# Retention, softplus layer and squared-ReLU layer on one core: the same chunk of two sequences in one visit

## The chip, the core and the metric

The kernel runs on one core of a Trainium2 chip. TensorE (PE) multiplies, VectorE (DVE), ScalarE (ACT) and GpSimd (POOL) work elementwise, and SyncE (SP) issues the DMAs. The metric is the device time of one execution in microseconds; the median of three runs before is 874.35 us.

## The reference

Three layers follow one another on 2304 tokens (4 sequences of 576) of width 512 (8 heads of 64).

```python
scores = scale * np.matmul(q, k.transpose(0, 1, 3, 2))       # (4, 8, 576, 576)
gamma = 1.0 - 2.0 ** (-5.0 - np.arange(H, dtype=np.float32))
Dmat = np.where(rel >= 0, gamma[:, None, None] ** rel[None, :, :], 0.0)
x = np.matmul(scores * Dmat, v)                              # then (2304, 512)
h = x @ w_in                                                 # w_in 512 x 2048
g = np.maximum(h, 0.0) + np.log1p(np.exp(-np.abs(h)))
x = g @ w_out                                                # w_out 2048 x 512
h = x @ w_in2
r = np.maximum(h, 0.0)
out = (r * r) @ w_out2
```

## The kernel before

**Retention.** Each sequence has 9 chunks of 64 tokens, 36 in all. A chunk tile `ch` holds q, k and v in three slots of 128 partitions: on the lower half (LO) q and k with the head's 64 dimensions on partitions and, in the third slot, the state; on the upper half (HI) k and v with tokens on partitions, and the masked products in the first slot. `step_s` (line 317) makes for each of 8 heads two 64x64 products: pb = k q (line 326; contraction over rows LO, output on columns HI) and, but for a sequence's last chunk, the running state st += k v (line 332; rows HI, columns LO). DVE masks pb into the chunk tile (line 336), ACT copies the state to the next chunk's tile (line 338). `step_o` (line 340) makes po of the same 8 heads (line 348), over all 128 rows, with even heads on columns LO and odd heads on HI, and DVE multiplies it with the decay table xw (line 361). A 64x64 product stands as two records of PE in the trace. The quadrant of a product follows from the partitions of its operands and of its output: rows LO or HI, columns LO or HI.

**First layer.** Tokens are cut into five tiles of 512, 384, 512, 512 and 384. A step is one of 16 blocks of w_in: `g1` (12 matmuls into a PSUM bank ph, line 401), softplus on ACT (lines 415 to 417) and DVE (lines 422, 425, 428, the last one reads ph), the split of its result (lines 437, 438), and two steps later `g2` (12 matmuls, line 453). During the steps of a tile, `attend` (line 757) visits the chunks of the next tile: one visit is step_o of the chunk before, the load of a chunk ahead, step_s of this chunk and the scaling of a loaded v (line 311). It stands between g1 of a step and g2 of an earlier one. The weights are converted on ACT and DVE (lines 140, 141, 145, 173, 174), all of the first layer's during the first tile, the second layer's w_in later.

**Start.** The chunks of tile 0 and one more are worked off before the first g1, in the order in which the code is written (`manual_schedule`, line 717); elsewhere a scheduler orders the instructions of each engine, and the engines take them in that order. PSUM has eight banks: four `ps_acc`, two `ps_h` (ph by turns), one `ps_at` (po), one `ps_st`. In the steady visits pb and st lie in the one bank of ps_st, pb on partitions HI and st on LO (line 324).

**Second layer.** From about 480 us on (lines 545 and 564), it reads the first layer's result back from DRAM and writes 18 output tiles of 128x512 (line 464).

## Time and profile before

| | |
|---|---|
| runs | 874.32, 874.35, 878.71 us; median 874.35 |
| span of the profiled execution | 871.7 us, 2.65 below the median; its own time outside the span is not recorded |
| PE busy | 858.3 us (98%) |
| DVE, ACT, POOL busy | 579.7, 422.2, 8.8 us |
| chain that ended last | PE 83%, DMA 6%, DVE 4%, ACT 4% |
| po, pb and st | 576, 576 and 512 records |

The span runs from the first to the last instruction. Busy time is the union of an engine's instructions, so a PE that is busy may still hold short matmuls that follow one another at less than its best pace; for them the starts in the timeline say more than the busy share. A record of a 512-wide matmul is longer (0.39 us) than the distance to the next start, since matmuls are pipelined.

### The profile page before, as it was taken

Reading aid. Unit: us, or ns where it says so; the run is one execution under the profiler, and the core shown is the slowest. Engines: PE = TensorE matmul, PEld = TensorE weight load, DVE = VectorE, ACT = ScalarE, POOL = GpSimd, SP = SyncE. Lnnn points to the kernel's source line nnn. Section 1 sums busy time; section 2 is a strip of 40 time slices with the busy share of each in tenths; the row PEclk is TensorE's granted clock in tenths of the full one; section 3 lists DMA queues with packets and bytes.
Section 4 is the critical chain, followed back from the end, with each engine's and each line's share of the span. In section 5 each row is a group of like instructions: output and inputs, shape, how many; then the busy total and the mean of one; then the engine's idle time right before and its main releaser. Section 6 shows DMA issues by size and latency. Waiting matters only on the chain.

```text
span 871.7 us, 14212 instructions
## 1 busy us (share of the span) xinstructions
PE 858.3 (98%) x5520; PEld 754.4 (87%) x5520; DVE 579.7 (67%) x1002; ACT 422.2 (48%) x763; POOL 8.8 (1%) x12
## 2 busy tenths in 40 slices
PE   8899999999999999999999999999999999999998
PEld 7777888999888888888999989888888988998896
DVE  3799899977896578745788874447645446553544
ACT  2599997665675446644696561213322113221121
POOL 2100000000000000000000000000000000000000
PEclk9999999999999999999999999999999999999999
DMA  9867764861583117610432464436644343644442
GB/s 209 229 181 211 220 210 148 246 203 50 165 264 104 30 45 239 221 36 1 170 115 55 149 226 121 120 110 193 193 115 115 121 118 115 191 120 115 116 121 85
DMA packets 75766, 126.32 MB, mean 145 GB/s; under 512 B 6706, under 2 KB 41650, under 8 KB 75698
## 3 DMA queue, kind: packets, MB, share of 16 engines
q1 hardware_dynamic: 75700, 125.42, 48.7%
q8 instruction: 44, 0.72, 0.3%
q14 instruction: 22, 0.18, 0.1%
HBM read 101.28 MB, written 24.12 MB: 144 GB/s over the span
## 4 chain that ended last, share of the span: by engine, by line
PE 83%; DMA 6%; DVE 4%; ACT 4%; issue 1%; SPq 0%; POOL 0%; DVEq 0%; ACTq 0%
PE acc L564 23%; PE acc L453 18%; PE ph L401 18%; PE py L545 9%; PE px L545 6%; PE pz L545 6%; PE st L326 2%; DMA wo_raw<-in_moe_w_out_dram 2%; DMA ch<-in_kv_dram 2%; PE po L348 2%; DMA wi_raw<-in_moe_w_in_dram 1%; DVE ct L145 1%; PE st L332 1%; DMA ch<-in_qk_t_dram 1%; ACT e L416 1%
## 5 line engine op out<-in xcount | busy, mean ns | idle before, releaser
L401 PE MATMUL ph<-xh,wi 128*128 128x512 f32 (+1 forms) x640 | 146.2, 369 | 2.9 <-DVE e L428 2.1
L401 PEld LDWEIGHTS ph<-xh,wi 128*128 128x128 f32 x640 | 116.3, 188 | 19.9 <-DVE e L428 2.2
L453 PE MATMUL acc<-gh,woh 128*128 128x512 f32 (+1 forms) x320 | 120.5, 378 | 0.0
L453 PE MATMUL acc<-gl,woh 128*128 128x512 f32 (+1 forms) x320 | 117.8, 368 | 0.2 <-DVE gl L438 0.2
L453 PE MATMUL acc<-gh,wol 128*128 128x512 f32 (+1 forms) x320 | 117.8, 368 | 0.0
L564 PE MATMUL acc<-woh,gring 128*128 128x512 f32 x288 | 104.9, 393 | 0.0
L545 PE MATMUL py<-t,sring 128*128 128x384 f32 x432 | 86.9, 335 | 0.3 <-DVE uring L652 0.3
L545 PEld LDWEIGHTS py<-t,sring 128*128 128x128 f32 x432 | 77.2, 188 | 6.8 <-DVE uring L652 0.6
L437 ACT CAST gh<-e 128x512 fp32r<-128x512 f32 (+1 forms) x80 | 45.8, 573 | 71.6 <-DVE e L428 54.2
L401 PE MATMUL ph<-xl,wi 128*128 128x512 f32 (+1 forms) x320 | 78.7, 367 | 0.0
L422 DVE SCALAR_TENSOR_TENSOR e<-e 128x512 f32<-128x512 f32 (+1 forms) x80 | 50.9, 636 | 38.0 <-ACT l L417 37.2
L438 DVE TENSOR_TENSOR gl<-e,gh 128x512 fp32r<-128x512 f32 (+1 forms) x80 | 50.9, 636 | 29.1 <-ACT gh L437 28.6
L453 PEld LDWEIGHTS acc<-gh,woh 128*128 128x128 f32 x320 | 60.0, 188 | 8.9 <-ACT gh L437 0.2
L453 PEld LDWEIGHTS acc<-gh,wol 128*128 128x128 f32 x320 | 60.1, 188 | 7.9
L590 ACT CAST gh<-g 128x384 fp32r<-128x384 f32 x48 | 24.6, 513 | 86.8 <-DVE g L577 72.1
L453 PEld LDWEIGHTS acc<-gl,woh 128*128 128x128 f32 x320 | 60.1, 188 | 7.5 <-DVE gl L438 0.4
L401 PEld LDWEIGHTS ph<-xl,wi 128*128 128x128 f32 x320 | 58.7, 188 | 7.6
L590 ACT CAST gring<-g 128x384 fp32r<-128x384 f32 x48 | 24.6, 513 | 83.0 <-DVE g L577 83.0
L415 ACT ACTIVATE e<-ph 128x512 f32<-128x512 f32 (+1 forms) x80 | 44.0, 550 | 37.3 <-PE ph L401 37.1
L564 PEld LDWEIGHTS acc<-woh,gring 128*128 128x128 f32 x288 | 54.0, 188 | 9.2
L545 PE MATMUL px<-t,sring 128*128 128x384 f32 x288 | 58.3, 337 | 0.0
L545 PE MATMUL pz<-t,sring 128*128 128x384 f32 x288 | 58.2, 337 | 0.0
...
## 6 DMA issues: line engine op xcount, KB each, us to landing
...
```

Of the source, the lines that this page charges most:

```text
L145: nc.vector.scalar_tensor_tensor(out=ct, in0=up, scalar=3, in1=low, op0=ALU.logical_shift_left, op1=ALU.bitwise_or,)
L326: nc.tensor.matmul(pb[HI, h, :], lhsT=kk[LO, h, :], rhs=qp[LO, h, :], start=True, stop=True, skip_group_check=True,)
L348: nc.tensor.matmul(po[(LO, HI)[h % 2], h // 2, :], lhsT=sv[rows, h, :], rhs=qp[rows, h, :], start=True, stop=True, skip_group_check=True,)
L401: nc.tensor.matmul(ph[:, :n], lhsT=a, rhs=x, start=(j == 0), stop=(j == len(todo) - 1))
L415: nc.scalar.activation(out=e, in_=ph[:, :n], func=AF.Abs)
L422: nc.vector.scalar_tensor_tensor(out=e, in0=e, scalar=-2.0, in1=e, op0=ALU.add, op1=ALU.mult)
L437: nc.scalar.copy(h[:, :n], g)
L438: nc.vector.tensor_tensor(out=l[:, :n], in0=g, in1=h[:, :n], op=ALU.subtract)
L453: nc.tensor.matmul(acc[j][:, :n], lhsT=a, rhs=x, start=(begin and m == 0), stop=(end and m == 2))
L545: nc.tensor.matmul(ps, lhsT=a, rhs=x, start=(first and m == 0), stop=(m == len(todo) - 1), skip_group_check=True,)
L564: nc.tensor.matmul(acc2[j, m], lhsT=a, rhs=x, start=(begin and n == 0), stop=(end and n == 2))
L590: nc.scalar.copy(h, g)
```

## The change

A visit takes chunk c of sequences 2s and 2s+1 together, so there are 18 visits, and the tokens stand in that order (64 of one sequence, 64 of the other) through both layers; each output tile is put back by two DMAs of 64 rows. The chunk tile has both sequences side by side, the load buffers are two pairs in place of three chunks. step_s splits the heads: heads 0 to 3 give pb on columns HI and st on LO, heads 4 to 7 pb on LO and st on HI, so that the four kinds of products lie on four quadrants. The state fills its bank; pb goes to the bank that the next ph will have (`pb_next`), in the start to one of ps_acc. Mask and state copy are two instructions of 64x512 per pair. The table xw is no longer made for all chunks at the start but just before each step_o (`make_xw`, into `xw_now`).

```diff
--- before.py
+++ after.py
@@ -18,7 +18,7 @@
 D = 64
 CN = 64
 SCN = 9
-LOADS = 3
+LOADS = 2
 STAGES = 3
 EARLY = {"wi": 9, "wo": 8}
...
@@ -89,20 +91,20 @@
     ew = ctx.enter_context(tc.tile_pool(name="ew", bufs=2))
     gp = ctx.enter_context(tc.tile_pool(name="gp", bufs=2))
     at = ctx.enter_context(tc.tile_pool(name="at", bufs=LOADS))
-    n_first = TILES[0][1] // CN
+    n_first = TILES[0][1] // P
     first = tc.tile_pool(name="first", bufs=n_first)
     first_pool = first.__enter__()
     late_wts = []
     ps_acc = ctx.enter_context(tc.tile_pool(name="ps_acc", bufs=4, space=PSUM))
-    ps_h = ctx.enter_context(tc.tile_pool(name="ps_h", bufs=2, space=PSUM))
+    ps_h = ctx.enter_context(tc.tile_pool(name="ps_h", bufs=1, space=PSUM))
     ps_at = ctx.enter_context(tc.tile_pool(name="ps_at", bufs=1, space=PSUM))
     ps_st = ctx.enter_context(tc.tile_pool(name="ps_st", bufs=1, space=PSUM))
     dram = ctx.enter_context(tc.tile_pool(name="dram", bufs=1, space=DRAM))
-    cst = const.tile([P, C_ALL], F32, name="cst")
+    cst = const.tile([P, C_T + 4 * (SCN - 1)], F32, name="cst")
     below_one = cst[:, C_ONE:C_ONE + 1]
     round_up = cst[:, C_UP:C_UP + 1]
-    mask = cst[CN:P, C_MASK:C_MASK + CN].unsqueeze(1).to_broadcast([CN, H, CN])
+    mask = cst[:, C_MASK:C_MASK + CN].unsqueeze(1).to_broadcast([P, H, CN])
     x2d = dram.tile([KD, P, NT], F32, name="x2d")
     NP = KF // 2
     KH = KD // 2
@@ -290,82 +292,113 @@
     LO, HI = slice(0, P // 2), slice(P // 2, P)
+    def place(c, s):
+        return (c // SCH * 2 + s) * SCH + c % SCH
+
+    def new_chunk(c):
+        if c < NPR:
+            pool = first_pool if c < n_first else at
+            chunk[c] = pool.tile([P, 3, 2, H, CN], F32, tag="ch", name="ch")
+
     def load_qk(c):
-        if c < NCH:
-            pool = first_pool if c < n_first else at
-            chunk[c] = pool.tile([P, 3, H, CN], F32, tag="ch", name="ch")
-            nc.sync.dma_start(out=chunk[c][LO, 0:2], in_=qk_t[c])
+        if c < NPR:
+            if c not in chunk:
+                new_chunk(c)
+            for s in range(2):
+                nc.sync.dma_start(out=chunk[c][LO, 0:2, s], in_=qk_t[place(c, s)])
     def load_kv(c):
-        if c < NCH:
-            nc.sync.dma_start(out=chunk[c][HI, 1:3], in_=kv[c])
+        if c < NPR:
+            for s in range(2):
+                nc.sync.dma_start(out=chunk[c][HI, 1:3, s], in_=kv[place(c, s)])
     def load_chunk(c):
         load_qk(c)
         load_kv(c)
     def scale_v(c, eng=nc.vector):
-        if c < NCH:
+        if c < NPR:
             t = chunk[c][HI, 2]
             w = cst[HI, C_VW + c % SCH * H:C_VW + (c % SCH + 1) * H]
             eng.tensor_tensor(
-                out=t, in0=t, in1=w.unsqueeze(2).to_broadcast([CN, H, D]), op=ALU.mult
+                out=t, in0=t, op=ALU.mult,
+                in1=w.unsqueeze(1).unsqueeze(3).to_broadcast([CN, 2, H, D]),
             )
     state = []
-
-    def step_s(c, split):
+    HH = H // 2
+
+
+
+
+    def step_s(c, pb):
         qp, kk, sv = (chunk[c][:, i] for i in range(3))
         go_on = c % SCH < SCH - 1
         if c % SCH == 0:
-            state[:] = [ps_st.tile([P, H, D], F32, tag="st", name="st")]
+            state[:] = [ps_st.tile([P, 2, HH, D], F32, tag="st", name="st")]
         st = state[0]
-        pb = st if not split else ps_acc.tile([P, H, CN], F32, tag="at", name="pb")
-        for h in range(H):
-            nc.tensor.matmul(
-                pb[HI, h, :], lhsT=kk[LO, h, :], rhs=qp[LO, h, :],
-                start=True, stop=True, skip_group_check=True,
-            )
-            if go_on:
-
-                nc.tensor.matmul(
-                    st[LO, h, :], lhsT=kk[HI, h, :], rhs=sv[HI, h, :],
-                    start=c % SCH == 0 and h == 0, stop=True, skip_group_check=True,
-                )
-        nc.vector.tensor_tensor(out=qp[HI], in0=pb[HI], in1=mask, op=ALU.mult)
+        for s in range(2):
+            for h in range(HH):
+                for to, hh in ((HI, h), (LO, h + HH)):
+                    nc.tensor.matmul(
+                        pb[to, s * HH + h, :], lhsT=kk[LO, s, hh, :], rhs=qp[LO, s, hh, :],
+                        start=True, stop=True, skip_group_check=True,
+                    )
+                if go_on:
+                    for to, hh in ((LO, h), (HI, h + HH)):
+                        nc.tensor.matmul(
+                            st[to, s, h, :], lhsT=kk[HI, s, hh, :], rhs=sv[HI, s, hh, :],
+                            start=c % SCH == s == h == 0, stop=True, skip_group_check=True,
+                        )
+        for of, i in ((HI, 0), (LO, 1)):
+            nc.vector.tensor_tensor(
+                out=qp[HI, :, i * HH:(i + 1) * HH],
+                in0=pb[of].rearrange("p (s h) c -> p s h c", s=2),
+                in1=mask[of].rearrange("p (s h) c -> p s h c", s=2), op=ALU.mult,
+            )
         if go_on:
-            nc.scalar.copy(chunk[c + 1][LO, 2], st[LO])
+            for of, i in ((LO, 0), (HI, 1)):
+                nc.scalar.copy(chunk[c + 1][LO, 2, :, i * HH:(i + 1) * HH], st[of])
+
+    def pb_acc():
+        return ps_acc.tile([P, H, CN], F32, tag="at", name="pb")
     def step_o(c, ps):
         qkv = chunk.pop(c)
         qp, sv = qkv[:, 0], qkv[:, 2]
         rows = slice(0, P) if c % SCH else HI
-        xw = cst[:, C_XW + c % SCH * 256:C_XW + (c % SCH + 1) * 256]
-        xw = xw.rearrange("p (a b) -> p a b", a=KD)
-        po = ps.tile([P, H, CN], F32, tag="at", name="po")[:, 0:KD, :]
-        for h in range(H):
-            nc.tensor.matmul(
-                po[(LO, HI)[h % 2], h // 2, :], lhsT=sv[rows, h, :], rhs=qp[rows, h, :],
-                start=True, stop=True, skip_group_check=True,
-            )
-        t, off = tile_of(c * CN)
+        xw = xw_first if c % SCH == 0 else xw_now
+        xw = xw.rearrange("p (a b) -> p a b", a=KD).unsqueeze(1).to_broadcast([P, 2, KD, CN])
+        po = ps.tile([P, H, CN], F32, tag="at", name="po").rearrange(
+            "p (s a) b -> p s a b", s=2
+        )
+        if c % SCH:
+            make_xw(c % SCH)
+        for s in range(2):
+            for h in range(H):
+                nc.tensor.matmul(
+                    po[(LO, HI)[h % 2], s, h // 2, :], lhsT=sv[rows, s, h, :],
+                    rhs=qp[rows, s, h, :], start=True, stop=True, skip_group_check=True,
+                )
+        t, off = tile_of(c * P)
         m = off // CN
         if t == 0:
-            x = ew.tile([P, 512], F32, tag="l", name="x")[:, :KD * CN]
-            x = x.rearrange("p (a b) -> p a b", a=KD)
+            x = ew.tile([P, 512], F32, tag="l", name="x")
+            x = x.rearrange("p (s a b) -> p s a b", s=2, a=KD)
         else:
             if t not in x_raw:
                 x_raw[t] = xs.tile([P, 512 // CN, KD, CN], F32, tag="xr", name="xr")
-            x = x_raw[t][:, m]
+            x = x_raw[t][:, m:m + 2]
         nc.vector.tensor_tensor(out=x, in0=po, in1=xw, op=ALU.mult)
         if t == 0:
-            cols = slice(off, off + CN)
-            nc.scalar.copy(x_hi()[:, :, cols], x)
-            nc.vector.tensor_tensor(
-                out=x_lo()[:, :, cols], in0=x, in1=x_hi()[:, :, cols], op=ALU.subtract
-            )
+            h, l = (
+                o[:, :, off:off + P].rearrange("p a (s b) -> p s a b", s=2)
+                for o in (x_hi(), x_lo())
+            )
+            nc.scalar.copy(h, x)
+            nc.vector.tensor_tensor(out=l, in0=x, in1=h, op=ALU.subtract)
     tick = [0]
@@ -387,8 +420,20 @@
     tmp = {}
     gg = {}
+    n_h = [0]
+
+
+
+    def h_bank(name, turn=True):
+        t = ps_h.tile([P, 512], F32, tag=f"h{n_h[0] % 2}", name=name)
+        n_h[0] += turn
+        return t
+
+    def pb_next():
+        return h_bank("pb", False).rearrange("p (h c) -> p h c", c=CN)
+
     def g1(key, f, n):
-        ph = ps_h.tile([P, 512], F32, tag="h", name="ph")
+        ph = h_bank("ph")
         wh, wl = w_hi[0, "wi", f], w_lo[0, "wi", f]
         todo, rest = [], []
         for kk in range(KD):
...
@@ -566,7 +613,11 @@
             )
         if end:
             t0 = b * PAIR + j * HALF + m * P
-            drain_one(j * MH + m, acc2[j, m], out[t0:t0 + P, :], DM)
+            dsts = []
+            for s, rows in enumerate((LO, HI)):
+                r0 = place(t0 // P, s) * CN
+                dsts.append((rows, out[r0:r0 + CN, :]))
+            drain_one(j * MH + m, acc2[j, m], dsts, DM)
     n_g = [0]
...
@@ -708,8 +758,8 @@
         nc.vector.scalar_tensor_tensor(
-            out=later[:, m - 1],
-            in0=cst[:, x_first].rearrange("p (a b) -> p a b", a=KD), scalar=float(D) ** 0.5,
+            out=xw_now.rearrange("p (a b) -> p a b", a=KD),
+            in0=xw_first.rearrange("p (a b) -> p a b", a=KD), scalar=float(D) ** 0.5,
             in1=times[:, m - 1].unsqueeze(2).to_broadcast([P, KD, CN]),
             op0=ALU.mult, op1=ALU.mult,
         )
@@ -722,17 +772,20 @@
                 out=rows_in[row:row + 1], in_=consts[row:row + 1, C_XW:]
             )
         load_chunk(0)
-        nc.sync.dma_start(out=cst[:, :C_XW], in_=consts[:, :C_XW])
+        for half in (LO, HI):
+            nc.sync.dma_start(out=cst[half, :C_XW], in_=consts[CN:P, :C_XW])
         for c in range(1, last + 1):
             load_chunk(c)
-            if c == last - 4:
+            if c == last - 2:
                 pump_load(1)
             elif c == last - 1:
                 pump_load(3)
+        new_chunk(last + 1)
         keep_warm(8)
         row = rows_in.rearrange("p (m a b) -> p m a b", a=KD, b=CN)
         spread(
-            cst[:, x_first].rearrange("p (a b) -> p a b", a=KD), row[:, 0], (KD, CN), nc.scalar.copy
+            xw_first.rearrange("p (a b) -> p a b", a=KD),
+            row[:, 0], (KD, CN), nc.scalar.copy,
         )
         spread(times, row[:, 1:, :, 0], (SCN - 1, KD), nc.scalar.copy)
         keep_warm(4)
@@ -740,18 +793,17 @@
             scale_v(c, nc.vector if c == last - 1 else nc.gpsimd)
             if c < last:
                 keep_warm(1)
-                step_s(c, True)
+                step_s(c, pb_acc())
                 if c:
                     step_o(c - 1, ps_acc)
-                make_xw(c + 1)
-                if c >= last - 3:
+                for _ in range((0, 0, 1, 2)[c]):
                     pump_step()
         keep_warm(2)
         step_o(last - 1, ps_acc)
         keep_warm(6)
     first.__exit__(None, None, None)
     late_wts.append(ctx.enter_context(tc.tile_pool(name="late", bufs=1, reuse_waits="tile")))
-    step_s(last, False)
+    step_s(last, pb_acc())
     tick[0] = last + 1
     def attend(b, f):
@@ -763,8 +815,8 @@
                 c = tick[0]
                 step_o(c - 1, ps_at)
                 load_chunk(c - 1 + LOADS)
-                if c < NCH:
-                    step_s(c, False)
+                if c < NPR:
+                    step_s(c, pb_next())
                 scale_v(c - 1 + LOADS)
                 tick[0] += 1
```

The order of instructions shows the change at three places. First TensorE, a visit in the second tile; L401 is g1, L453 g2. Before:

```order
L401 MATMUL ph<-xh,wi_1181 128x384 x8
L401 MATMUL ph<-xl,wi_1181 128x384 x4
L348 MATMUL po<-ch 64x64 x8
L326 MATMUL st<-ch 64x64
L332 MATMUL st<-ch 64x64
```

The last two rows come eight times each by turns, then g2 follows. In the changed program L446 is g1, L380 po, L344 pb, L350 st, L498 g2:

```order
L446 MATMUL ph<-xh,wi_998 128x384 x8
L446 MATMUL ph<-xl,wi_998 128x384 x4
L380 MATMUL po<-ch 64x64 x16
L344 MATMUL pb<-ch 64x64 x2
L350 MATMUL st<-ch 64x64 x2
```

The rows of step_s come eight times each, two products at a time: the two of a pair lie on the two column halves, and pb and st on the two row halves. Pairs 7 and 9 to 16 stand like this. In pair 8 the 16 pb (it has no st) are parted from po and cut by matmuls of g1, and in pair 17 the 16 pb follow po.

Second TensorE at the beginning of the first tile, where the scheduler fills the first g1 steps with the visits of the next chunks. Before:

```order
L401 MATMUL ph<-xl,wi_439 128x512 x4
L348 MATMUL po<-ch 64x64 x8
L326 MATMUL st<-ch 64x64
L401 MATMUL ph<-xh,wi_439 128x512 x6
L332 MATMUL st<-ch 64x64
```

After:

```order
L344 MATMUL pb<-ch 64x64 x4
L380 MATMUL po<-ch 64x64
L446 MATMUL ph<-xh,wi_393 128x512 x8
L446 MATMUL ph<-xl,wi_393 128x512 x4
L380 MATMUL po<-ch 64x64 x11
L344 MATMUL pb<-ch 64x64 x8
L350 MATMUL st<-ch 64x64 x16
L380 MATMUL po<-ch 64x64 x3
L446 MATMUL ph<-xh,wi_393 128x512 x8
L446 MATMUL ph<-xl,wi_393 128x512 x4
L380 MATMUL po<-ch 64x64
```

Here pb and st of a pair follow one another and don't alternate; further pieces of po, of 7 and 5 products, stand later between g1 and g2.

Third DVE at the end of the start, from the scaling of the last chunk of tile 0 (before L311, after L323) to the x that the first g1 reads. L336 and L355 are masks, L361 and L393 x, L366 and L401 xl, L710 and L760 xw, L145 and L147 a conversion. Before:

```order
L311 TENSOR_TENSOR ch<-ch,cst 64x512
L145 SCALAR_TENSOR_TENSOR ct<-wi_raw 128x512
L336 TENSOR_TENSOR ch<-pb,cst 64x512
L361 TENSOR_TENSOR x<-po,cst 128x256
L174 TENSOR_TENSOR wi_439<-ct,wi_439 128x512
L366 TENSOR_TENSOR xl<-x,xh 128x4x64
L710 SCALAR_TENSOR_TENSOR cst<-cst,times 128x256
L174 TENSOR_TENSOR wi_439<-ct,wi_439 128x512
L361 TENSOR_TENSOR x<-po,cst 128x256
```

After:

```order
L323 TENSOR_TENSOR ch<-ch,cst 64x1024
L355 TENSOR_TENSOR ch<-pb,cst 64x2x256 x2
L760 SCALAR_TENSOR_TENSOR xw_now<-cst 128x256
L393 TENSOR_TENSOR x<-po,xw_now 128x512
L401 TENSOR_TENSOR xl<-x,xh 128x2x4x64
L147 SCALAR_TENSOR_TENSOR ct<-wi_raw 128x512 x3
L176 TENSOR_TENSOR wi_393<-ct,wi_393 128x512
L760 SCALAR_TENSOR_TENSOR xw_now<-cst 128x256
L355 TENSOR_TENSOR ch<-pb,cst 64x2x256
L393 TENSOR_TENSOR x<-po,xw_now 128x512
```

The scaling came after one conversion and before two others; now all three conversions stand behind it, and so does the whole work of two pairs.

## Rows read from the trace of the kernel before

**Rows 1.** Busy time by stretch: length, then PE, PEld, DVE, ACT, POOL, PEclk, DMA.
```profile
46.00:134.60 88.60, 86.92 (x549) 70.13 (x545) 81.52 (x135) 85.84 (x153) 0.00 (x0) 1.00 0.67 198
134.60:415.00 280.40, 280.40 (x2121) 241.25 (x2122) 207.52 (x359) 165.24 (x289) 0.00 (x0) 1.00 0.45 136
```

**Rows 2.** Timeline of PE, 228.5 to 246: start, length, instruction, count.
```profile
230.51 2.01 PE L401 MATMUL ph<-xh,wi 128*128 128x512 f32 x8
...
235.99 1.98 PE L401 MATMUL ph<-xh,wi 128*128 128x512 f32 x8
...
238.80 0.69 PE L348 MATMUL po<-ch 128*64 128x64 f32 x16
239.42 0.27 PE L326 MATMUL st<-ch 64*64 64x64 f32 x1
239.42 0.27 PE L332 MATMUL st<-ch 64*64 64x64 f32 x1
...
240.49 0.50 PE L453 MATMUL acc<-gh,woh 128*128 128x512 f32 x1
```

**Rows 3.** Timeline of PE, 248 to 257, around a sequence's last chunk.
```profile
248.81 1.98 PE L401 MATMUL ph<-xh,wi 128*128 128x512 f32 x8
...
251.62 0.69 PE L348 MATMUL po<-ch 128*64 128x64 f32 x16
252.24 1.14 PE L326 MATMUL st<-ch 64*64 64x64 f32 x16
253.31 0.50 PE L453 MATMUL acc<-gh,woh 128*128 128x512 f32 x1
...
256.18 1.07 PE L401 MATMUL ph<-xh,wi 128*128 128x512 f32 x4
```

**Rows 4.** Timeline of PE, 35.3 to 46.5, where po and pb meet.
```profile
44.59 0.51 PE L348 MATMUL po<-ch 64*64 64x64 f32 x10
...
44.99 0.22 PE L326 MATMUL st<-ch 64*64 64x64 f32 x1
44.99 0.28 PE L348 MATMUL po<-ch 64*64 64x64 f32 x3
```

**Rows 5.** Groups of DVE's instructions by form: busy us, mean ns, idle before.
```profile
L336 DVE TENSOR_TENSOR ch<-st,cst 64x512 f32<-64x512 f32 x28 | 19.5, 695 | 6.6 <-PE st L332 4.3 <-PE st L326 1.6
...
L361 DVE TENSOR_TENSOR xr<-po,cst 128x256 f32<-128x256 f32 x28 | 11.8, 420 | 3.3 <-PE po L348 3.1
```

**Rows 6.** Timeline of POOL, 0 to 47: scaling of chunks 5 and 6.
```profile
21.23 1.04 POOL L311 TENSOR_TENSOR ch<-ch,cst 64x512 f32<-64x512 f32 x1 [4.48 <-DMA ch<-in_kv_dram]
23.53 1.04 POOL L311 TENSOR_TENSOR ch<-ch,cst 64x512 f32<-64x512 f32 x1 [1.25 <-DMA ch<-in_kv_dram]
```

**Rows 7.** Timeline of all engines, 30 to 37.
```profile
30.21 0.69 DVE L311 TENSOR_TENSOR ch<-ch,cst 64x512 f32<-64x512 f32 x1
...
36.52 0.73 PE L401 MATMUL ph<-xh,wi 128*128 128x512 f32 x2
```

**Rows 8.** Timeline of all engines, 96 to 105, a visit in the first tile.
```profile
99.31 0.69 PE L348 MATMUL po<-ch 128*64 128x64 f32 x16
...
101.18 0.69 DVE L428 SCALAR_TENSOR_TENSOR e<-ph,l 128x512 f32<-128x512 f32 x1
...
102.83 0.69 DVE L336 TENSOR_TENSOR ch<-st,cst 64x512 f32<-64x512 f32 x1
...
103.88 1.29 PE L401 MATMUL ph<-xh,wi 128*128 128x512 f32 x5
```

**Rows 9.** Timeline of DVE, 250 to 255, the visit of rows 3.
```profile
250.39 0.68 DVE L428 SCALAR_TENSOR_TENSOR e<-ph,l 128x512 f32<-128x512 f32 x1
...
253.41 0.69 DVE L336 TENSOR_TENSOR ch<-st,cst 64x512 f32<-64x512 f32 x1 [0.21 <-PE st L326]
```

**Rows 10.** Timeline of SP, 862 to 872.
```profile
864.98 4.01 SPq L464 DMA_DIRECT2D out_dram<-xo  x6
```

32 lines of the change are left out of this document (17 added, 15 removed).

## The prediction

> **What bounds the kernel now.** I read the busy time by stretch first, then TensorE's own timeline around single visits of the retention, and last the queues of VectorE and ScalarE beside them. From the second token tile on, 134.60 to 415.00 us, PE is busy all of the 280.40 us, at the full granted clock (2.4 GHz), while DVE has 207.52 and ACT 165.24 [rows 1]. A microsecond of TensorE that goes there is a microsecond of the span, as long as nobody else becomes late. The first tile is another matter: of 88.60 us ACT is busy 85.84, DVE 81.52, PE 86.92 [rows 1]. There three engines are nearly full, and ACT has 2.76 us left.
>
> What a visit costs TensorE is read by comparing two steps. A step of one g1 and one g2 without a visit goes from 230.51 to 235.99, 5.48 us [rows 2]. One with a visit goes from 248.81 to 256.18, 7.37 us [rows 3]. So a visit costs 1.89 us: the block of po, 0.62 (251.62 to 252.24), the block that starts with pb, 1.07 (252.24 to 253.31), and 0.20 of slower neighbours.
>
> The key reading is that the pb/st block takes 1.07 us in both forms. At 252.24 the last chunk of a sequence runs 16 records, pb alone, on one quadrant [rows 3]. At 239.42 an ordinary chunk runs 32, pb on rows LO and st on rows HI, started together, and the next 512-wide matmul stands at 240.49, again 1.07 us later [rows 2]. What limits is the quadrant: one record every (1.14 - 0.22)/15 = 0.061 us [rows 3, 4]. A second quadrant beside it is free. A third is seen too: at 44.99 a record of L326 (rows LO, columns HI) starts within the same 10 ns as records of L348 that alternate between both column halves of rows HI [rows 4]. The fourth is not in this trace.
>
> **The change part by part.** *Full visits.* Each takes two sequences, so two visits become one. po has 32 records, spaced (0.69 - 0.22)/15 = 0.031 us [rows 3, 4]: 0.62 + 16 x 0.031 = 1.12 us. pb and st have 64, in 16 rounds of four quadrants. If all four run beside each other the block stays at 1.07; if only two do, 16 more rounds of 0.061 make it 2.05. I take 1.07: the row nearest to it has three quadrants free of charge. With 0.20 for the neighbours a full visit costs 2.39 where two cost 3.78.
>
> A rule of the Trainium skill speaks of this place. The two lines of 239.42 write the same tile st, hence one bank, from two row halves, at no cost [rows 2]. "TensorEngine Tiling (Array Packing)", section "Gotcha 1: PSUM Pressure", says that different row tiles can't access one PSUM bank at the same time. By it the block before would hold about 2.05 us, not 1.07, and giving pb a bank of its own would win 0.98 more per visit; the row is against it, and I count nothing.
>
> *The sum from 134.60 on.* Before: 21 visits (chunks 15 to 35) and a last po: 21 x 1.89 + 0.82 = 40.5 us. After, by the order of the instructions: pairs 9 to 16 and 17 are whole (17 has pb alone, 32 records on two quadrants, again 16 rounds): 9 x 2.39 = 21.5. Pair 8 is cut in three pieces by g1 matmuls. An extra piece costs at most what of a visit is neither po nor pb records, 1.89 - 16 x 0.031 - 16 x 0.061 = 0.42, so 2.39 + 0.8 = 3.2. The last po: 1.12 + 0.20 = 1.3. Together 26.0. Saved 14.5 us, or 14.5 - 8 x 0.98 = 6.7 with two quadrants.
>
> *First tile.* PE saves here too: three visits in place of six. But ACT's work doesn't shrink: the state is still two copies of 64x512 per pair, and conversion and softplus are untouched. With 2.76 us of ACT left, the gain lies between 0 and 2.76. I take 0.5, near nothing, because the pieces there (the order shows po in fragments of 11, 3, 1, 7 and 5) cost 0.42 each and pb is new to wait, below.
>
> *Start.* The input of tile 0 comes at the pace of the loads: kv of chunk 5 was there at 21.23, of chunk 6 at 23.53 [rows 6], so of chunk 7 near 25.8, and pair 3 at the same time, as the same bytes stand ahead of it. Before, DVE scaled chunk 7 at 30.21 and the first g1 began at 36.52 [rows 7]. After, DVE has, from the scaling of pair 3 to the x that g1 waits for, as the order gives them: scaling of 1024 columns 1.38 (twice 0.69 [rows 7]), three masks of 0.70 [rows 5], two x at 0.69 (the size of [rows 8]), xl 0.69, two xw of 128x256 at about 0.42 [rows 5], three conversions and one wi at 0.69: 1.38 + 2.10 + 1.38 + 0.69 + 0.84 + 2.76 = 9.2 us, from 25.8 to 35.0, then the cast on ACT, under 0.7. Free of waits g1 starts at 35.7, 0.8 us earlier than before. But inside this row xl waits for a cast that now stands behind the conversion of the third weight on ACT, and the second mask of the next pair waits for TensorE. One wait as long as three DVE instructions, 2.1 us, makes it 1.3 later, two make it 3.4. Bounds -1 and +5, value +2, since both waits are visible in the order.
>
> *New wait.* pb moves out of st's bank into the bank of the next ph. That bank is free when DVE has done L428 of the step before, and the next g1 must wait for the masks, now two. In the third tile L428 ended at 251.07, before po began at 251.62 [rows 3, 9], and the mask ended at 254.10 where g1 came at 256.18; with 0.70 + 0.27 more for the second mask and the wider x [rows 5], 1.1 us are left: free. In the first tile L428 ended at 101.87, po began at 99.31 and ends after 1.12, so pb would wait 1.4 us; the mask ended at 103.52 and g1 began at 103.88 [rows 8]: 0.36 - 0.97, so 0.6 us more. In the second tile DVE lies between these. Behind a waiting pb the whole of g2 is queued. Between 0 and 2.0 us for each of four visits (pairs 8 to 11); I take 0.25 each, 1.0. In the first tile ACT hides it.
>
> *Hidden at nothing.* The loads: the same 72 issues of the same size, two pairs ahead in place of three chunks; a pair lands in 4 x 1.15 = 4.6 us (half of 2.30 per kind [rows 6]), and visits lie 20 us apart. The xw table is now made in 16 visits, not 8 at the start: 16 x 0.42 on DVE, which has 72.9 us idle from 134.60 to 415.00 [rows 1]. Uncovered, both would cost under 1 us a visit. *End.* Each output tile is written by two DMAs; six issues with their waits took 4.01 us before [rows 10], so one more behind the last is at most 0.67: +0.4.
>
> Total: -14.5 - 0.5 + 2 + 1.0 + 0.4 = -11.6 us on the span of 871.7, so 860.1. The median of the runs, 874.35, lies 2.65 above that span; I carry it: **862.7 us**.
>
> **The rivals.** *Two quadrants at a time.* For: no stretch of the trace holds more than three, and over a whole block records never came closer than 1.07/32 = 0.033 us. Against: [rows 4]. It adds 7.8: 870.5. The Trainium skill has a rule of that kind: "TensorE: Matmul & The Clock Gate", section "Wait — 56ns, not 53.3ns?", puts the spacing of starts at 25 ns or more however short the matmul. By that figure 64 records would take 1.6 us, an estimate from the page, and the kernel about 867; the starts at 44.99 lie closer, but only for three records.
>
> *The first tile gives its share.* ACT loses its 2.76 us of waits and the start isn't later: 874.35 - 14.5 - 2.76 + 0.4 = 857.5. For: ACT's idle time there is mostly waiting for others. Against: three static queues.
>
> *pb waits for the bank* (slower side). If DVE lags in every visit as at 99.31, each of the 13 visits after the start loses 1.4 + 0.6 = 2.0 us: 862.7 - 1.0 + 26 = 887.7. For: DVE was late by this much in the first tile, and 69% to 92% busy everywhere before 415. Against: [rows 9]. It turns the sign when the loss in each exceeds 12.6/13 = 1.0 us.
>
> **How the numbers follow.** Forecast 0.60, two quadrants 0.16, first tile too 0.12, the bank 0.08, and 0.04 for a start over 5 us late. The likeliest gives 862.7. Its own bounds: start -1 to +5, waits 0 to 8, first tile 0 to 2.76: about 858 to 869. The range takes in the two-quadrant case and most of the first-tile case: 856 to 871. What this kernel's runs can tell from no change is 0.5%, 4.4 us: faster is below 870.0, slower above 878.7. Faster: 0.58 of the forecast, half of the two quadrants, 0.12 of the first tile: 0.78. Slower: 0.05, most of the bank's case. Same: 0.17.
>
> **What would show it.** Right: a full visit of the third tile with 64 records in 1.07 us between po and the next g2, four starting together; a step with a visit of 5.48 + 2.39 = 7.87. Two quadrants: 5.48 + 3.37 = 8.85. The start: the first g1 between 35.5 and 41. The bank: idle PE before pb, released by DVE's softplus line, or before g1, released by a mask. The first tile: its end, the first g1 of the second tile, against 134.6. I am wrong if the saved time from 134.60 to 415.00 isn't near 14 us, or if the first tile loses more than 5.

## The result and the profile after

The changed kernel takes 886.67 us (median of 4 runs, 882.77 to 891.07); the kernel before took 876.53 us beside it. The ratio is 1.0119, 95% interval 1.0093 to 1.0144: slower, where I forecast 862.7. The profiled execution took 886.12 us with a span of 884.4, 12.7 us more than before. The first g1 of each tile shows where:

| | before | after | difference |
|---|---|---|---|
| first g1 | 36.52 | 44.29 | +7.8 |
| first g1 of tile 2 | 133.02 | 148.53 | +15.5 |
| first g1 of tile 5 | 415.74 | 424.87 | +9.1 |
| last matmul begins | 867.34 | 876.59 | +9.3 |
| end | 871.7 | 884.4 | +12.7 |

So the start loses 7.8, the first tile 7.7 more, tiles 2 to 4 win back 6.4 (14.5 less 1.0 of waiting were forecast), and the end loses 3.4. In the changed kernel g1 is L446, g2 L498, po L380, pb L344, st L350, the masks L355, x L393, the casts of x L400 and L401, the scaling of V L323.

The busy time by stretch (start and end in us, length, then PE, PEld, DVE, ACT, POOL, clock, DMA) answers to [rows 1]:

```profile
44.30:148.50 104.20, 98.05 (x623) 78.44 (x623) 88.62 (x141) 90.22 (x159) 0.00 (x0) 0.95 0.71 188
148.50:424.90 276.40, 269.63 (x2082) 231.05 (x2081) 207.37 (x351) 164.91 (x290) 0.00 (x0) 1.00 0.47 137
```

From 134.60 to 415.00 PE had no idle time before [rows 1]; now 6.8 of 276.4 us are idle. PE's timeline at a full visit of the third tile answers to [rows 2, 3]:

```profile
278.02 1.15 PE L380 MATMUL po<-ch 128*64 128x64 f32 x32
279.10 0.27 PE L344 MATMUL pb<-ch 64*64 64x64 f32 x2
279.11 0.27 PE L350 MATMUL st<-ch 64*64 64x64 f32 x2
...
280.19 0.50 PE L498 MATMUL acc<-gh,woh 128*128 128x512 f32 x1
...
283.79 0.47 PE L446 MATMUL ph<-xh,wi 128*128 128x512 f32 x1 [0.56 <-DVE ch L355]
```

Four records start within 10 ns, and 64 take 1.09 us (279.10 to 280.19): the four quadrants run beside each other. The blocks of po, pb and st take 2.17 us (278.02 to 280.19), 2.19 were forecast. But g1 stands behind a mask. The waits of PE in tiles 2 to 4 (total, times, longest) are two lines, and neither stands there before:

```profile
PE ph L446 <- DVE ch L355: 6.2, 8, 1.2
PE pb L344 <- DVE e L473: 0.5, 2, 0.3
```

Such a wait costs more than its idle time: this step lasts 8.58 us from g1 to g1 (275.21 to 283.79) and the next one 5.56, together 0.8 more than the 7.87 and 5.48 forecast, for a wait of 0.56. Over eight waits that is about 2 us, an estimate from this visit. The 14.5 us less 6.8 of waits and these 2, and with a wait of 0.7 that the kernel before had at 133 us, come to the 6.4 measured.

DVE's timeline at that visit says why the mask is late; it answers to [rows 9]:

```profile
279.75 0.68 DVE L393 TENSOR_TENSOR xr<-po,xw_now 128x512 f32<-128x512 f32 x1
280.46 0.43 DVE L760 SCALAR_TENSOR_TENSOR xw_now<-cst 128x256 f32<-128x256 f32 x1
280.81 0.68 DVE L467 SCALAR_TENSOR_TENSOR e<-e 128x512 f32<-128x512 f32 x1
281.52 0.69 DVE L470 SCALAR_TENSOR_TENSOR l<-e,l 128x512 f32<-128x512 f32 x1
282.25 1.39 DVE L355 TENSOR_TENSOR ch<-pb,cst 64x512 f32<-64x512 f32 x2
```

pb was there at 280.2, but DVE's order has the next xw and two instructions of softplus ahead of the masks; they begin 2 us later. At 235, 304 and 334 us the same three instructions stand between x and the masks. In the kernel before, at the visit of [rows 9], the mask came right behind x, ahead of softplus:

```profile
252.79 0.41 DVE L361 TENSOR_TENSOR xr<-po,cst 128x256 f32<-128x256 f32 x1
253.41 0.69 DVE L336 TENSOR_TENSOR ch<-st,cst 64x512 f32<-64x512 f32 x1 [0.21 <-PE st L326]
254.14 0.69 DVE L145 SCALAR_TENSOR_TENSOR ct<-wi_raw 128x512 uint32<-128x512 uint32 x1
254.75 0.69 DVE L422 SCALAR_TENSOR_TENSOR e<-e 128x512 f32<-128x512 f32 x1
```

The start is read from the timeline of DVE, 28 to 33, of all engines, 33 to 45, and of PE:

```profile
28.11 1.22 DVE L323 TENSOR_TENSOR ch<-ch,cst 64x1024 f32<-64x1024 f32 x1 [0.95 <-DMA ch<-in_kv_dram]
31.27 1.41 DVE L355 TENSOR_TENSOR ch<-pb,cst 64x512 f32<-64x512 f32 x2 [1.93 <-PE pb L344]
```

```profile
33.44 0.68 ACT L142 ACTIVATE wi_raw<-wi_raw 128x512 f32<-128x512 f32 x1 [2.15 <-DMA wi_raw<-in_moe_w_in_dram]
...
34.79 1.17 ACT L362 COPY ch<-st 64x512 f32<-64x512 f32 x2
35.86 0.62 ACT L400 CAST xh<-x 128x512 fp32r<-128x512 f32 x1
36.51 0.69 DVE L401 TENSOR_TENSOR xl<-x,xh 128x512 fp32r<-128x512 f32 x1 [2.46 <-ACT xh L400]
36.72 2.25 POOL L323 TENSOR_TENSOR ch<-ch,cst 64x1024 f32<-64x1024 f32 x1 [15.45 <-DMA ch<-in_kv_dram]
37.12 3.60 DVE L147 SCALAR_TENSOR_TENSOR ct<-wi_raw 128x512 uint32<-128x512 uint32 x3
```

```profile
44.29 3.78 PE L446 MATMUL ph<-xh,wi 128*128 128x512 f32 x8
```

Pair 3 is there at 28.1, not at 25.8 as forecast, and its masks wait 1.93 for TensorE. The cast of x stands on ACT behind the third weight, whose load it waits for; DVE waits 2.46 for the cast; then three conversions take 3.60 beside the scaling on POOL, where one took 0.69. The eight matmuls of g1 take 3.78 us, about twice the usual 2.0, at a low clock. The stretches 5:10, 10:15 and 40:45 of the changed kernel, then the first two of the kernel before (PE busy second, clock third from last):

```profile
5.00:10.00 5.00, 1.83 (x20) 1.51 (x16) 0.00 (x0) 0.46 (x2) 0.11 (x1) 1.00 1.07 214
10.00:15.00 5.00, 3.10 (x66) 2.57 (x66) 1.28 (x2) 1.12 (x2) 2.36 (x2) 0.60 1.07 212
...
40.00:45.00 5.00, 2.66 (x34) 2.01 (x27) 4.88 (x9) 4.38 (x8) 0.00 (x0) 0.67 0.85 234
```

```profile
5.00:10.00 5.00, 4.33 (x56) 3.33 (x54) 1.16 (x2) 1.04 (x3) 2.08 (x2) 1.00 1.03 230
10.00:15.00 5.00, 4.99 (x115) 4.41 (x116) 3.18 (x7) 1.93 (x4) 2.09 (x2) 1.00 1.03 223
```

PE now idles for the larger first pair, and then the granted clock is 0.60 of 2.4 GHz, partly at the 1.2 GHz level. In the first tile PE stands twice, 2.11 and 2.58 us, because DVE stands behind a load:

```profile
93.39 1.22 DVE L323 TENSOR_TENSOR ch<-ch,cst 64x1024 f32<-64x1024 f32 x1 [1.86 <-DMA ch<-in_kv_dram]
...
128.44 1.22 DVE L323 TENSOR_TENSOR ch<-ch,cst 64x1024 f32<-64x1024 f32 x1 [2.15 <-DMA ch<-in_kv_dram]
```

```profile
95.99 3.53 PE L446 MATMUL ph<-xh,wi 128*128 128x512 f32 x8 [2.11 <-DVE e L473]
130.53 3.62 PE L446 MATMUL ph<-xh,wi 128*128 128x512 f32 x8 [2.58 <-DVE e L473]
```

Each of these waits is paid a second time: the eight matmuls behind it take 3.53 and 3.62 us where 1.98 is usual, and the granted clock of the stretch is 0.66, partly at the 1.2 GHz level. Here are the two stretches, then the whole first tile before, in the change, and in run 8 (below), which has the same work there but for some 14 records, and a clock of 1.00:

```profile
95.00:100.00 5.00, 4.01 (x11) 3.15 (x12) 5.00 (x9) 3.95 (x7) 0.00 (x0) 0.66 0.39 111
130.00:135.00 5.00, 4.47 (x13) 3.62 (x14) 4.81 (x9) 4.68 (x9) 0.00 (x0) 0.66 0.47 116
```

```profile
36.52:133.02 96.50, 95.45 (x650) 76.79 (x649) 88.29 (x143) 90.09 (x160) 0.00 (x0) 1.00 0.70 205
44.29:148.53 104.24, 98.09 (x624) 78.45 (x623) 88.66 (x141) 90.26 (x159) 0.00 (x0) 0.95 0.71 188
49.59:148.09 98.50, 93.71 (x608) 74.65 (x609) 88.25 (x140) 89.48 (x158) 0.00 (x0) 1.00 0.75 196
```

The 7.7 us of the first tile are thus 5.1 us more of waiting (6.2 against 1.0), and PE busy for 2.6 us more although three visits stand there in place of six. At a clock of 1.00 PE is busy 1.7 us less than before. So some 4.4 us go with the lower clock, an estimate from these rows, since run 8 enters the tile 5.3 us later.

At the end SyncE issues twelve DMAs one after the other, which answers to [rows 10]:

```profile
874.23 7.54 SPq L510 DMA_DIRECT2D out_dram<-xo  x12
```

### The profile page after: what moved, and what is told of

Same layout as the page of the kernel before. It is cut to its first block, busy times and chain, and to the rows that moved or that the text cites. A ratio compares the mean times of both kernels' runs of the same rounds, so it can differ in the third digit from the quotient of the medians.

```text
span 884.4 us, 14178 instructions
## 1 busy us (share of the span) xinstructions
PE 848.1 (96%) x5512; PEld 744.7 (84%) x5512; DVE 577.6 (65%) x974; ACT 421.8 (48%) x759; POOL 8.2 (1%) x8
## 2 busy tenths in 40 slices
DMA packets 80678, 126.32 MB, mean 143 GB/s; under 512 B 7010, under 2 KB 41954, under 8 KB 80610
## 4 chain that ended last, share of the span: by engine, by line
PE 65%; DMA 12%; DVE 12%; ACT 7%; issue 2%; SPq 2%; DVEq 0%; ACTq 0%
PE acc L611 22%; PE ph L446 12%; PE acc L498 9%; PE py L592 8%; DMA ch<-in_kv_dram 7%; PE px L592 6%; PE pz L592 6%; DMA wi_raw<-in_moe_w_in_dram 3%; DMA wo_raw<-in_moe_w_out_dram 2%; DVE ct L147 2%; DVE e L473 1%; DVE l L470 1%; DVE e L467 1%; DVE ch L323 1%; DVE ch L355 1%
## 5 line engine op out<-in xcount | busy, mean ns | idle before, releaser
L446 PE MATMUL ph<-xh,wi 128*128 128x512 f32 (+1 forms) x640 | 152.1, 380 | 12.3 <-DVE ch L355 6.2
L446 PEld LDWEIGHTS ph<-xh,wi 128*128 128x128 f32 x640 | 118.6, 193 | 34.3 <-issue 5.0
L498 PE MATMUL acc<-gh,woh 128*128 128x512 f32 (+1 forms) x320 | 118.7, 372 | 0.0
L498 PE MATMUL acc<-gl,woh 128*128 128x512 f32 (+1 forms) x320 | 117.9, 368 | 0.0
L498 PE MATMUL acc<-gh,wol 128*128 128x512 f32 (+1 forms) x320 | 117.8, 368 | 0.0
L446 PE MATMUL ph<-xl,wi 128*128 128x512 f32 (+1 forms) x320 | 79.5, 369 | 0.0
L498 PEld LDWEIGHTS acc<-gh,woh 128*128 128x128 f32 x320 | 60.0, 188 | 8.1
L498 PEld LDWEIGHTS acc<-gl,woh 128*128 128x128 f32 x320 | 60.1, 188 | 7.7 <-DVE gl L483 0.3
L498 PEld LDWEIGHTS acc<-gh,wol 128*128 128x128 f32 x320 | 60.1, 188 | 7.7
L446 PEld LDWEIGHTS ph<-xl,wi 128*128 128x128 f32 x320 | 59.5, 190 | 8.1
```

What stands on the lines that cost most here:

```text
L446: nc.tensor.matmul(ph[:, :n], lhsT=a, rhs=x, start=(j == 0), stop=(j == len(todo) - 1))
L498: nc.tensor.matmul(acc[j][:, :n], lhsT=a, rhs=x, start=(begin and m == 0), stop=(end and m == 2))
```

## The experiments

The theory: the quadrants' gain is real and is lost in four places, the bank that the masks hold (A), DVE's queue behind loads (B), the order of the start (C) and the end (D). The rival throughout: DVE's pace as a whole sets the time, whatever is moved. The before of the five groups of runs was at 876.2 to 877.2 us, so medians are compared; the ratio is to before. Places inside a run are read from its one traced execution, and the first tile differs between executions: run 3 has the change's program up to its outputs, and its second tile begins at 151.53, 3.0 later, at a granted clock of 0.91 in the first tile where the change had 0.95. A few us in the first tile can be the clock's and not the edit's.

| run | median | ratio, 95% |
|---|---|---|
| the change | 886.67 | 1.0119 (1.0093 to 1.0144) |
| 1 banks swapped | 879.74 | 1.0036 (1.0018 to 1.0055) |
| 2 scaling on GpSimd | 889.67 | 1.0143 (1.0120 to 1.0166) |
| 3 output on two queues | 885.55 | 1.0089 (1.0056 to 1.0122) |
| 4 chunk layout | 887.76 | 1.0104 (1.0071 to 1.0137) |
| 5 one sequence, first form | 883.96 | 1.0088 (1.0063 to 1.0112) |
| 6 two quadrants | 885.72 | 1.0104 (1.0063 to 1.0146) |
| 7 pair 4 first | 886.73 | 1.0121 (1.0066 to 1.0175) |
| 8 warm matmuls | 885.63 | 1.0106 (1.0079 to 1.0134) |
| 9 order of the start | 881.83 | 1.0055 (1.0035 to 1.0076) |
| 10 late scaling | 889.61 | 1.0123 (1.0074 to 1.0173) |
| 11 three edits | 874.36 | 0.9979 (0.9960 to 0.9997) |
| 12 four edits | 877.22 | 0.9997 (0.9979 to 1.0015) |
| 13 one sequence, second form | 878.86 | 1.0022 (1.0005 to 1.0039) |
| 14 two quadrants, banks swapped | 881.68 | 1.0062 (1.0043 to 1.0080) |
| 15 weights' order | 877.00 | 1.0014 (0.9994 to 1.0033) |
| 16 one DMA per output | 939.70 | 1.0725 (1.0701 to 1.0748) |
| 17 no scaling | 883.64 | 1.0065 (1.0048 to 1.0083) |
| 18 no scaling, three edits | 872.49 | 0.9942 (0.9926 to 0.9959) |

**A. The bank: runs 1, 6, 14.** Run 1 exchanges the banks of po and pb:

```
-                step_o(c - 1, ps_at)
+                step_o(c - 1, None)
-                    step_s(c, pb_next())
+                    step_s(c, ps_at.tile([P, H, CN], F32, tag="at", name="pb"))
...
+        if ps is None:
+            po = h_bank("po", False).rearrange("p (h c) -> p h c", c=CN)
```

> Theory (the masks hold the bank that the next g1 needs, 7.5 us lost at eight g1 of tiles 2 to 4): with po in the bank of the next ph and pb in the bank that po had, g1 waits for x alone, which DVE does before the masks. The waits of g1 on the mask line vanish and the kernel falls by 5 to 8 us, to 879 to 882. Rival (DVE is late as a whole in these steps, the bank is only where it shows): po then waits for the softplus line of the step before, or g1 for x, by about as much as g1 waited for the masks, and the time stays at 885 to 888.

6.9 us less, but not as I thought. g1's wait for the masks is gone from tiles 2 to 4; there stands instead, in its trace:

```profile
PE po L382 <- DVE e L475: 4.6, 5, 2.1
```

po waits for softplus of the step before. Tiles 2 to 4 take 274.2 us (276.3 in the change), and the first tile ends at 141.63, not 148.53. This trace is of the fastest of ten executions, 2.8 under the median, at a clock of 0.99 in the first tile, so how much of the 6.9 falls where stays open. A visit that waits for nothing shows the forecast step: 7.86 us from g1 to g1 (291.85 to 299.71; 7.87 forecast). Theory and rival each hold in part. Run 6 writes all pb ahead of all st:

```
+        for s in range(2):
+            for h in range(HH):
                 if go_on:
```

> The changed kernel with all pb products of a visit ahead of all st products, so that no more than two quadrants can run beside each other. Theory (the gain of the four quadrants is real and is seen in the kernel's time wherever TensorE is the bound): the pb and st block goes from 1.07 to about 2.05 us, 8 full visits of tiles 2 to 4 cost 7.8 us more, the first tile adds 0 to 5: 894 to 899. Rival (the block is not what the visit costs there, DVE's masks are): the visits lose nothing on the whole and the time is 885 to 889.

The block is longer, as expected in kind: a full visit costs 3.15 us, 0.76 more. Yet the time is the same, and in its trace the masks' wait is down to

```profile
PE ph L448 <- DVE ch L357: 0.2, 1, 0.2
```

PE is busy 272.6 us of tiles 2 to 4 (269.6 in the change), and its waits fall from 6.8 to 0.6, so the stretch takes 273.1 us where the change took 276.3. (The eight longer visits are worth 8 x 0.76 = 6.1 us; 38 records of a po stand in the first tile here, and the waits' further cost is gone.) What PE saved by the quadrants it stood before the next g1, and more. Run 14 repeats it with the banks exchanged.

> po in the bank of the next ph and pb in po's bank (alone 879.74), and all pb products ahead of all st products, so that two quadrants run beside each other at most. Theory (with the masks no longer holding g1, what the four quadrants save in a visit, 0.76 us as measured in the run without the bank's edit, is seen in the time): 8 full visits of tiles 2 to 4 and some of the first tile, 885 to 888. Rival (DVE's pace sets these tiles in either form): 878 to 881.

881.68 against 879.74, between the two; tiles 2 to 4 take 277.2, 3.0 more than in run 1. Half of what two quadrants cost is now seen, the rest is still covered by waits for DVE, 3.0 us in place of 5.1. DVE is busy 207 of the 276 us of tiles 2 to 4 in the change, which speaks against its pace as a whole and for what stands in its order at these places.

**B. DVE's queue: runs 2, 10, 17, 18.** Run 2 moves the scaling of the steady visits to GpSimd (`scale_v(c - 1 + LOADS, nc.gpsimd)`).

> Theory (DVE stands behind the scaling of V, which waits for a pair's load, and the two stalls of TensorE in the first tile at 93.5 and 127.6, 2.3 and 2.7 us, come from that): with the scaling of the steady visits on GpSimd both stalls go, 4 to 5 us, so 881 to 883. Rival (a GpSimd instruction beside DVE slows DVE, as at 37.1 where an instruction of 0.69 took 2.40): each of the 14 scalings makes DVE late by 1 us or more, the masks and so g1 come later, and the time is 889 or more.

The rival's side: the first tile ends at 147.19, 1.3 earlier, but tiles 2 to 4 take 283.1 us, 6.7 more. The groups of DVE in 134:430 (busy, mean ns) in the change and in run 2:

```profile
L467 DVE SCALAR_TENSOR_TENSOR e<-e 128x512 f32<-128x512 f32 (+1 forms) x52 | 33.6, 647 | 35.8 <-ACT l L462 35.2
...
L147 DVE SCALAR_TENSOR_TENSOR ct<-wi_raw 128x512 uint32<-128x512 uint32 x17 | 11.6, 684 | 0.0
```

```profile
L467 DVE SCALAR_TENSOR_TENSOR e<-e 128x512 f32<-128x512 f32 (+1 forms) x50 | 36.3, 727 | 41.5 <-ACT l L462 41.2
...
L323 POOL TENSOR_TENSOR ch<-ch,cst 64x1024 f32<-64x1024 f32 x9 | 17.7, 1968 | 200.4 <-DMA ch<-in_kv_dram 120.9 <-ACT e L460 43.0 <-DMA s2d<-ct 19.9
...
L147 DVE SCALAR_TENSOR_TENSOR ct<-wi_raw 128x512 uint32<-128x512 uint32 x17 | 14.3, 844 | 0.0
```

Run 10 writes `scale_v(c)` at the head of the visit that uses it.

> The changed kernel with the scaling of V written at the head of the visit that uses it, not at the end of the visit before. Theory (DVE stands behind a scaling that waits for a pair's load at 93.4 and 128.4): both stalls go and the kernel gains 3 to 5 us, 882 to 884. Rival (the scaling, 1.2 us, now stands between TensorE's pb and st in every visit): TensorE waits for it at up to 14 visits, 1 us or more each, 890 or more.

The profiled execution ran at 881.44 with the first tile's end at 143.05; the other three were at 889 to 891. Inconclusive. Runs 17 and 18 drop `scale_v` from pair 5 on.

> The changed kernel without the scaling of V from pair 5 on (left out, so V is used as loaded): VectorE has 1.2 us less in each of 13 visits and no wait for a load in its queue. Theory (VectorE's queue at the visits is what TensorE waits for): the two stalls of the first tile (5.0) and most of the 6.2 us of waiting for the masks go, 875 to 879. Rival (the bank or the loads hold TensorE whatever VectorE does): 884 to 888.

> The three edits together (874.36) without the scaling of V from pair 5 on (left out, so V is used as loaded). Theory (VectorE's queue): 4 to 8 us less, 866 to 870, which is near what I had forecast for the change. Rival (with po and pb in their new banks VectorE is no longer waited for): 872 to 875.

3.0 and 1.9 us less: run 17 is at the rival's lower end, run 18 inside the rival's range. In run 17 the two stalls shrink from 4.7 to 0.6 us, so they were the scaling's; its first tile ends at 144.58, 4 earlier, at a clock of 0.97. But the masks' wait in tiles 2 to 4 is 7.2 us, no smaller. Of my theory for B only the first tile's part stands.

**C. The start: runs 4, 7, 8, 9, 15.** Run 4 makes the sequence the outer index of the chunk tile (`[P, 2, 3, H, CN]`).

> Theory (part of the late start and of the late loads in the first tile comes from the destination's two pieces of 2 KB per partition instead of one of 4 KB): with the sequence as the outer index of the chunk tile a load's packets fall back to those of the kernel before, the median landing of kv goes from 6.0 to about 5 us, pair 3 lands at about 26 and not 28.0, the first g1 comes 1 to 2 us earlier than 44.29 and the kernel is at 883 to 885. Rival (landing goes by bytes and by what stands in the queue): landings within 0.3 us of those now, 886 to 887.

Packets fall from 80678 to 76071, kv lands after 5.9 us (6.0) and the first g1 is at 43.84: the pieces' size does not set the landing here. Run 7 loads pair 4 ahead of weights 1 and 2 and takes two conversion steps behind the last x; run 8 has more idle matmuls (`keep_warm((24, 12, 4, 30)[c])`).

> The changed kernel with pair 4 loaded ahead of the second and third weight, and these two converted after the last x of the start. Theory (the late start is in the order: x of pair 3 stands on ScalarE and DVE behind weight conversions that wait for their loads, and the scaling of pair 4 on GpSimd falls beside DVE's conversions): the first g1 comes at 39 to 41, not 44.3, and the kernel is at 881 to 884. Rival (the first tile is bound by ScalarE's and DVE's work and the weights' arrival, not by where it begins): the second tile begins at 148.5 as now and the time stays at 885 to 888.

> The changed kernel with 66 more idle matmuls of 128x128 in the start, where TensorE waits for the scaling of pairs 0, 1 and 3. Theory (the start is also slow because TensorE idles 5.0 us for pair 0 where it idled 0.3 before, after which the granted clock of 10 to 45 us is 0.5 to 0.8): the granted clock of 10 to 40 us is at 0.95 or more, the first g1 comes 0.5 to 1 us earlier and the kernel is at 882 to 885. Rival (the start waits for loads and DVE, and TensorE's pace there costs nothing): first g1 at 44.3 and 886 to 888, or later where the added matmuls stand in the way.

Neither moves the time. In run 7 the cast of x still waited for weight 2 (first g1 at 42.86). In run 8 one block of warm matmuls lasted 8.57 us and put the first g1 at 49.59, but its first tile, at a clock of 1.00, takes 98.5 us, 5.7 less than in the change, and the second tile begins at 148.09. What the clock alone costs at the start stays open, and the clock row doesn't tell it: in the traces of runs 1 and 10 it is 1.00 from 10 to 40 us and 0.66 in the change, yet pair 3's block of pb and st takes 1.9 to 2.0 us in all three, and the first g1 is at 44.03, 44.31 and 44.29. Run 9 writes both later weights behind the last x:

```
-            elif c == last - 1:
+            elif c == last:
                 pump_load(3)
...
         step_o(last - 1, ps_acc)
+        pump(2)
```

> The changed kernel with pair 4 loaded ahead of weights 1 and 2, and the conversion of these two written behind the last x of the start, so that on ScalarE the casts of x for pairs 2 and 3 no longer stand behind activations that wait for a weight's load. Theory (the late start is this order: the cast of x stood behind the third weight's load, DVE's conversion of weight 0 behind that cast, and SyncE's next loads behind that conversion's buffer): the first g1 comes at 38 to 40, the second at 43 to 46 (53.7 now), the second tile begins at 140 to 143 and the kernel is at 877 to 881. Rival (the first tile is bound by the work of ScalarE, so a start earlier by some us is waited away): the second tile begins at 146 or later and the time is 884 or more.

4.8 us less. ACT's timeline now has the cast before the weight:

```profile
39.75 0.62 ACT L400 CAST xh<-x 128x512 fp32r<-128x512 f32 x1 [0.21 <-DVE x L393]
40.27 0.68 ACT L142 ACTIVATE wi_raw<-wi_raw 128x512 f32<-128x512 f32 x1
```

The first g1 is at 40.75, the second tile at 143.69 and the time 881.83, each just short of the theory's figure. C is shown for 3.5 of the start's 7.8 us.

**Together: runs 11, 12, 15, and the end (D): runs 3, 16.** Run 3 issues the second half of each output tile from ScalarE (`zip((nc.sync, nc.scalar), dsts)`).

> Theory (the end is 3.4 us longer because SyncE issues twelve output DMAs of 64 rows, about 0.6 us each, one after the other): with the second half of each tile issued from ScalarE's queue the last issue stands some 2 us earlier after the last copy, and the kernel is at 884 to 885. Rival (the end is the landing of the last bytes or the copies, not the issue): no change, 886 to 887, or the copies on ScalarE come later by the issues that stand ahead of them.

From the last matmul to the end it takes 6.1 us instead of 7.8, but the whole difference, 1.1, is within the intervals. Run 11 has the edits of 1, 3 and 9; run 12 also that of 10.

> Three edits together: po in the bank of the next ph and pb in po's (-6.9 alone, measured), the second half of each output tile issued by ScalarE (-1.1 alone, measured), and the new order of the start (as in the run of that edit alone, expected -6 to -9). Theory (they are separate places and add): 871 to 875, and the start at 38 to 40. Rival (the first two tiles have one bound, so what the start gains the bank's edit had already taken): 877 to 880.

> The same three edits and the scaling of V at the head of the visit that uses it. Theory (the stalls at 93 and 128 are DVE's queue behind a load): 3 to 5 us less than the run without it, 867 to 871, with two stalls of TensorE in the first tile gone. Rival (st waits for the scaling in each visit): slower than the run without it by 3 or more.

Run 11 is the version that beats both: 874.36, ratio to before 0.9979 with its interval just below 1. Its first tile ends at 141.33 and tiles 2 to 4 take 274.4. With the late scaling it is 2.9 slower, near the rival's 3. Runs 15 and 16 start from run 11: run 15 loads weight 1 ahead of pair 4 again, and run 16 besides writes each output tile by one DMA on SyncE that strides over the two sequences.

> The three edits together (874.36 alone), with weight 1 loaded ahead of pair 4 and weight 2 behind it. Theory (the third g1, at 52.47 with 2.2 us of waiting for the conversion of weight 2, is late by the load's order): the third g1 at 49 to 51, 872 to 874. Rival (pair 4 lands later and its state and masks wait): first or second g1 later by 1 us or more, 874 to 877.

> As the run with the weights' order, but each output tile is written by one DMA whose destination strides over the two sequences, all on SyncE. Theory (the end is longer by the second issue of each tile): from the last matmul to the end 4.4 to 5 us as in the kernel before, instead of 6.1, so 1 to 2 us less than the run with two queues. Rival (the end is the landing of the 64-row pieces): no change against that run.

Run 15 went the rival's way: the third g1 is at 57.22, not 49 to 51. Run 16 was a large miss: 62.7 us more than run 15. DVE waited for those DMAs to free their buffers, and SyncE's last six issues took 20.18 us:

```profile
DVE g L628 <- DMA out_dram<-xo: 33.1, 4, 8.7
```

```profile
902.58 20.18 SPq L512 DMA_DIRECT2D out_dram<-xo  x6
```

**Pairs or quadrants: runs 5 and 13.** The kernel before, with one sequence per visit, its own loads of the chunks and its own end, one more load of the mask at the start, and from chunk 9 on

```
+        for h in range(HH):
+            for to, hh in ((HI, h), (LO, h + HH)):
...
+                for to, hh in ((LO, h), (HI, h + HH)):
```

In run 5 pb lies in po's bank, in run 13 in the bank of the next ph.

> The kernel before, with one sequence per visit, its own start and its own end; only from chunk 9 on pb and st are spread over four quadrants (pb in the second half of po's bank). Theory (the quadrants give the gain, the double visits with their start, loads and outputs take it back): the first g1 stays at 36.5, a visit falls from 1.89 by 8 rounds of 0.061 to about 1.40, 21 visits from the second tile on give 10.3 us, and the kernel is at 864 to 868, faster than both. Rival (the gain is eaten wherever it is made, because DVE and ScalarE now have two masks and two copies of 64x256 per visit where they had one of 64x512): DVE is late for the next g1 and the kernel is at 872 or more.

> The kernel before with one sequence per visit and its own start, loads and end; from chunk 9 on pb and st are spread over four quadrants, pb in the bank of the next ph. Theory (the loss is the pairs', the quadrants gain): first g1 at 36.5 to 38, visits of 1.40 to 1.45 from the second tile on instead of 1.89, no wait of g1 for the masks longer than 0.3, so tiles 2 to 4 take 273 to 276 us instead of 282.7 and the kernel is at 866 to 870. Rival (two masks and two copies per visit, 36 times, are what DVE and ScalarE can't carry): g1 or pb waits for DVE by 0.3 us or more per visit, the kernel is at 873 to 880.

Both missed. In run 5 pb was placed apart from st (16 records of pb begin 1.74 us after st's in the third tile), so it shows nothing of four quadrants: tiles 2 to 4 take 288.9 us, 6.2 more than before, and the first g1 is at 40.98. In run 13 a visit of the third tile costs 1.46 us instead of 1.89, yet tiles 2 to 4 take 279.0 us instead of 282.7, with 4.3 us of PE's waits for softplus ahead of pb. Its first g1 is at 39.52, 3.0 later than before, and its first tile ends at 143.18, which makes it 7.2 longer than before, with 4.7 us of waits and a clock of 0.97. So the pairs are not the whole loss: the quadrants alone, in this order of DVE, gain 3.7 of about 9 us in tiles 2 to 4 and lose as much in the first tile as the pairs do.

## Why the prediction was wrong

The span was to fall by 11.6 us and rose by 12.7. Of these 24.3 us the first tile has 8.2, tiles 2 to 4 have 7.1, the start 5.8 and the end 3.0. The sum's own bounds, added up, give 856 to 873 and not "about 858 to 869"; the result lies outside either.

- *Full visits: right.* 2.39 forecast; 2.17 for the blocks and, in run 1, a step of 7.86 measured; last po 1.3 as forecast; pair 8 3.2 in pieces as forecast, pair 17 2.6 beside its waits (2.39 forecast). "Two quadrants" as a rival is out, and with it the 25 ns between starts that the Trainium skill gives ("TensorE: Matmul & The Clock Gate", section "Wait — 56ns, not 53.3ns?"): 64 records in 1.09 us are one every 17 ns, and four of them start within 10.
- *New wait: this step failed first.* I wrote of the third tile "1.1 us are left: free". I took DVE's order from the kernel before, mask right behind x, and counted only longer instructions. In the changed order the next xw and two softplus instructions come between, and the wait is 6.2 + 0.5 us in tiles 2 to 4 where I had 1.0, and costs about 2 us more than its idle time. The rival "pb waits for the bank" named the right resource, but put 1.4 of its 2.0 us a visit on pb, which hardly waits; g1 does. That its time (887.7) is near is luck: it gave all of its 25 us to waits of visits, and start, first tile and end took most of them. Run 6 shows that this wait takes the quadrants' gain. That moving the masks ahead of softplus would free it is argued from the rows; it was not tried.
- *Start: this step failed as much.* +2 with a bound of +5; measured +7.8. I saw "xl waits for a cast that now stands behind the conversion of the third weight" and gave it 2.1 us by choice. It was 2.46. Not priced were pair 3's load (28.1, not 25.8), the masks' wait of 1.93 for TensorE, and the conversions slowed by POOL's larger scaling (3.60 for three where 2.07 was counted). Run 9 gets 3.5 us of the first g1 back by the order alone.
- *First tile: the sign was wrong.* -0.5 with a bound of 0 to -2.76; measured +7.7. I bounded it by ACT's idle time, as if a delay were impossible. Two terms stood at nothing. One is the loads, "the same 72 issues of the same size": a pair's kv lands after 6.0 us at the median, 4.9 before, DVE waits for it in its order and PE for DVE (4.7 us in two waits, 0.6 in run 17). The other is TensorE's clock, 0.95 in this tile and 1.00 before, worth some 4.4 us by the rows of run 8, against 1.7 that the fewer visits save. That the clock's part is as large is estimated, not shown by a run that changes it alone. Run 11 still takes 101.9 from first g1 to second tile, before 96.5: PE waits 6.2 us there and the clock is 0.97.
- *End: the term was mis-sized.* +0.4 forecast, +3.4 measured. I priced one more issue behind the last; all twelve stand in a row, 7.54 us. Run 3 recovers 1.7 in its trace.
- *What would make it wrong* was named: the saved time "isn't near 14" (it is 6.4) and "the first tile loses more than 5" (it loses 7.7).
